# Windowed attention and a softplus layer on one core: later blocks' scores in three matmuls per query tile, a corrected plan with a table of due times, and the last store in pieces

## The chip, the core and the metric

The kernel runs on one core of one Trainium2 chip. Five engines of that core work side by side and wait for each other through semaphores: TensorE (PE, matrix products; the loads of its stationary operand are shown apart as PEld), VectorE (DVE), ScalarE (ACT), GpSimd (POOL) and SyncE (SP, which here only issues DMAs). The metric is device time of one launch in microseconds (us); three runs of the kernel before have a median of 963.94 us.

## The reference

Attention in a sliding window of 64 keys for 8 batches x 8 heads x 576 positions x 64 dimensions, and behind it a layer with softplus between two weight matrices, on the 4608 rows of 512 that the attention gives:

```python
scores = (q @ k.T) / sqrt(64)                 # masked to 0 <= pos_q - pos_k < 64
attn = softmax(scores);  x = attn @ v         # x: 4608 x 512
h = x @ w_in                                  # 512 x 2048
g = maximum(h, 0) + log1p(exp(-abs(h)))
out = g @ w_out                               # 2048 x 512
```

The precision is that of fp32. Most products run in a faster form of fp32 (fp32r), and for that each operand is split in a high part (the value rounded to that form) and a low part (what is left of it); three products, high by high, high by low and low by high, stand for one.

## The kernel before, in words

**Tiling.** The 4608 rows are 12 blocks of 384 (`TB`), numbered `g` in the order in which they are worked. A block has four pairs of heads (`hp`) and three query tiles of 128 rows. The inner width of 2048 is 16 slices `f` of 128. There are 192 steps of the layer: block 0 with slices 0 to 7, block 1 with all 16, block 0 with the rest, and then each later block with all 16. A step is an up product U (12 matmuls of 384 columns, L622), ACT's three passes and DVE's one for softplus (L626 to L634), the split of the result in `g0` and `g1` (L636, L637), and a down product D (9 matmuls of 512 columns, L646), which adds into three PSUM banks `ps_o`. U has two PSUM banks (`ps_h`), so the U after the next can start only when DVE's L634 has read the bank of this one. "U4 of the second pass" below is U for block 1 and slice 4.

**Weights.** They arrive as 64-bit words, 1 MB for a slice. `convert` makes fp32 of them and splits it: ACT L297, DVE L298, L300, L302, ACT L304, DVE L305. All 16 slices are converted once, at the start.

**Attention.** Blocks 0, 1 and 2 take their scores in full fp32 straight from q and k as loaded (L367); for blocks 0 and 1, PE also turns the probabilities and multiplies them with v (L487, L498). Blocks 3 to 11 (36 pairs of heads, 108 query tiles) split q and k: `q_hl` holds q's high parts on partitions 0 to 63 and its low parts on 64 to 127; `k_s[0]` and `k_s[1]` hold k's high and its low parts, each twice, on both halves. A query tile then takes four matmuls of 192 columns (L411): for either head one with `k_s[0]` and one with `k_s[1]`. Behind the scores stand DVE's row minima (L338), ACT's exponentials with their sums (L436), DVE's division (L451), the split of the probabilities (L527 to L532), a DMA that turns them, and the product with v (L590).

**Order.** Nothing is left to a scheduler: `arrange` plays the whole program through with a cost for each operation, a due time for each, and rules for the buffers (each `Ring` has so many places; an operation that opens a buffer waits for the users of the one whose place it takes). Whatever comes out is the order in which every engine's instructions are written. `latest` then makes new due times from the end backwards, and the best of 8 rounds is kept. PE, DVE, ACT and POOL each take their instructions strictly in that order; SP's DMAs too.

**Start.** `setup` makes masks on POOL and DVE. For block 0, the first 64 columns of k are zeroed on POOL as part of the load (L354), behind POOL's own masks and its memset of `v13` (L274).

**End.** Each finished block is copied out of its three PSUM banks (L681) and stored in two pieces, 512 KB and 256 KB (L684).

Of the kernel before, what the change touches and what calls it, by code (L numbers as in the profile page):

```python
# [8 lines left out]
F32 = mybir.dt.float32  # L9
# [6 lines left out]
P = 128  # L16
# [10 lines left out]
ROUNDS = 8  # L27
DOWN = 6.3
AHEAD = (1, 1, 8, 8)
APART = (4, 6, 18, 19)  # L30
STRETCH = 1.4
EARLY = 30
# [4 lines left out]
RESULT = {"PE": 0.25, "DVE": 0.12, "ACT": 0.15, "POOL": 0.2, "SP": 2.0}  # L37
BYTES_PER_US = 390e3
LAUNCH = 1.3
# [30 lines left out]
def arrange(ops, rings):  # L70
# [3 lines left out]
    free = {"PE": 0.0, "DVE": 5.0, "ACT": 2.1, "POOL": 0.8, "SP": 0.8}  # L74
    pipe = 2.2
# [7 lines left out]
    while len(order) < len(ops):  # L83
        best = None
        for e, waiting in open_ops.items():
# [21 lines left out]
            o = min((o for at, o in could if at <= t + 1e-9), key=lambda o: o.due)  # L107
# [4 lines left out]
        t, o = best  # L112
        o.start = t
        free[o.eng] = t + o.cost
        o.end = t + o.cost + RESULT[o.eng]
        if o.nbytes:
            pipe = max(pipe, t + o.cost + LAUNCH) + o.nbytes / BYTES_PER_US
            o.end = pipe + RESULT["SP"]
# [7 lines left out]
        for n in o.later:  # L126
            left[id(n)] -= 1
            ready_at[id(n)] = max(ready_at[id(n)], t + o.cost if n.eng == o.eng and not o.nbytes else o.end)
            if not left[id(n)]:
                open_ops[n.eng].append(n)  # L130
# [44 lines left out]
def window_attention_softplus_ffn(  # L175
# [107 lines left out]
    converted = {}  # L283

    def convert(f):
# [9 lines left out]
        a = add("SP", 0.45, lambda: nc.sync.dma_start(raw(), w_words[f]), opens=[raw], nbytes=1024 * 1024, name=f"load{f}")  # L295
# [18 lines left out]
    def attention(g, hp):  # L314
# [27 lines left out]
        if quad:  # L342
# [9 lines left out]
            def load_k():  # L352
                if skip:
                    nc.gpsimd.memset(qk(1)[:, 0:CH], 0.0)  # L354
                by.dma_start(qk(1)[:, skip:], kT[c0 : c0 + P, t0 - CH + skip : t0 + TB])
            lq = add("SP", 0.65, lambda: nc.sync.dma_start(qk(0), qT[c0 : c0 + P, rows_t]), deps=waits, opens=[slot],
                     uses=[two["q_in"], two["k_in"], *far], nbytes=192 * 1024, name=f"q{tag}")
            lk = add("ACT" if by is nc.scalar else "SP", 0.65, load_k, deps=waits, opens=[],
# [22 lines left out]
        else:  # L381
# [7 lines left out]
            for i, half in enumerate(heads):  # L389
# [4 lines left out]
            k_s = [buf(att, [P, 2, CH + TB], F32R, f"k{i}") for i in range(2)]  # L394
# [4 lines left out]
            kh = add("ACT", 0.84, lambda: nc.scalar.copy(k_s[0](), k_in()), deps=loads[1], opens=[k_s[0]], uses=[k_in], name=f"kh{tag}")  # L399
            kl = add("DVE", 1.11, lambda: tt(k_s[1](), k_in(), k_s[0]().bitcast(F32), ALU.subtract), deps=[kh], opens=[k_s[1]],  # L400
                     uses=[k_in, k_s[0]], name=f"kl{tag}")
# [343 lines left out]
    with tc.manual_schedule():  # L745
        setup()
        for o, at in best[1]:
            o.fn()
# [44 lines left out]
```

## Time and profile before

| | |
|---|---|
| median of three runs (lowest, highest) | 963.94 us (963.61, 964.43) |
| the profiled execution: its own time | 965.21 us |
| the profiled execution: its span, first to last instruction | 963.4 us |
| mean granted TensorE clock | 0.993 |
| HBM over the span | 74.58 MB read, 10.22 MB written, 88 GB/s |

The span is shorter than the execution's own time by 1.8 us, which lie outside the recorded instructions. PE, DVE, ACT and POOL rows give busy time; "waits" give the time in which an engine sat idle and what ended it; the "chain that ended last" follows the program back from its last instruction, at each step to whatever released it. A busy PE is not PE at its peak, since matmuls are pipelined and their records overlap: the pace is read from the chain, whose pieces do not overlap. The rows themselves are shown in the prediction.

### The profile page before, as it was taken

The page shows a single profiled execution, that of the slowest core. Times are in us where ns is not written, and L with a number is a line of the kernel's source. Part 1 is how long each engine was busy: PE and PEld are TensorE (multiplying, and loading weights), DVE is VectorE, ACT ScalarE, POOL GpSimd, SP SyncE. Part 2 cuts the span into 40 slices and gives each one's busy share as a digit, 9 for nine tenths or more (in the row PEclk, how much of TensorE's full clock was granted, in tenths as well). Part 3 has the DMA queues.
Part 4 walks back from the last instruction along what each step waited for, and adds up shares of the span by engine and source line. Part 5 has one row for each costly group of instructions (what it writes and reads, how often), then busy time and mean ns, then how long its engine had stood idle before and what let it go on. Part 6 is the DMA issues. An engine that isn't in the chain of part 4 may idle for free.

```text
span 963.4 us, 16889 instructions
## 1 busy us (share of the span) xinstructions
PE 939.7 (98%) x6128; PEld 848.6 (88%) x6128; DVE 784.6 (81%) x1760; ACT 740.5 (77%) x1685; POOL 4.5 (0%) x18
## 2 busy tenths in 40 slices
PE   5899999999999999999999999999999999999997
PEld 4678888999999999998999999999999999998996
DVE  7999977898798888889879889879888887975333
ACT  6899877888788788778878778778878887875443
POOL 1000000000000000000000000000000000000000
PEclk7999999999999999999999999999999999999999
DMA  9961225575347345344445535535635464521000
GB/s 364 422 231 44 61 71 121 131 178 124 90 129 138 98 139 116 94 117 128 122 99 145 137 76 145 132 89 140 127 86 150 116 111 99 148 52 34 34 1 33
DMA packets 196516, 117.37 MB, mean 122 GB/s; under 512 B 130192, under 2 KB 187536, under 8 KB 194384
## 3 DMA queue, kind: packets, MB, share of 16 engines
q1 hardware_dynamic: 196144, 115.90, 46.0%
q8 instruction: 48, 0.79, 0.4%
q10 hardware_dynamic: 288, 0.39, 0.1%
q14 instruction: 36, 0.29, 0.1%
HBM read 74.58 MB, written 10.22 MB: 88 GB/s over the span
## 4 chain that ended last, share of the span: by engine, by line
PE 91%; DVE 6%; ACT 1%; issue 1%; POOL 0%; POOLq 0%; ACTq 0%
PE ps_o L646 40%; PE ps_h L622 40%; PE ps_a L590 6%; PE ps_a L411 5%; DVE work L300 1%; DVE work L302 1%; DVE w L305 1%; ACT st L436 1%; DVE st L338 1%; DVE work L298 1%; DVE u L634 0%; DVE g L637 0%; PE ps_a L367 0%; DVE st L451 0%; DVE x L505 0%
## 5 line engine op out<-in xcount | busy, mean ns | idle before, releaser
L622 PE MATMUL ps_h<-x,w 128*128 128x384 f32 x2304 | 435.2, 338 | 4.2 <-DVE u L634 3.2
L646 PE MATMUL ps_o<-w,g 128*128 128x512 f32 x1728 | 424.9, 394 | 0.0
L622 PEld LDWEIGHTS ps_h<-x,w 128*128 128x128 f32 x2304 | 401.9, 188 | 15.0 <-DVE u L634 3.9
L646 PEld LDWEIGHTS ps_o<-w,g 128*128 128x128 f32 x1728 | 320.3, 188 | 60.4 <-ACT u L626 0.2
L626 ACT ACTIVATE u<-ps_h 128x384 f32<-128x384 f32 x192 | 93.8, 488 | 138.2 <-PE ps_h L622 134.9
L634 DVE SCALAR_TENSOR_TENSOR u<-ps_h,u 128x384 f32<-128x384 f32 x192 | 106.3, 554 | 95.8 <-ACT u L628 93.5
L436 ACT ACTIVATE st<-st,mn 128x128 f32<-128x128 f32 x288 | 111.7, 389 | 24.2 <-DVE st L428 19.1
L637 DVE TENSOR_TENSOR g<-u,g 128x384 fp32r<-128x384 f32 x192 | 106.3, 554 | 10.1 <-ACT g L636 5.8
L628 ACT ACTIVATE u<-u 128x384 f32<-128x384 f32 x192 | 100.9, 525 | 6.1
L627 ACT ACTIVATE u<-u 128x384 f32<-128x384 f32 x192 | 100.8, 525 | 6.1
L338 DVE CUSTOM_DVE_ANT_0 st<-ps_a,wide 128x192 f32<-128x192 f32 x176 | 53.3, 351 | 13.8 <-PE ps_a L411 13.8
L636 ACT CAST g<-u 128x384 fp32r<-128x384 f32 x112 | 56.5, 505 | 9.8 <-DVE u L634 9.0
L590 PEld LDWEIGHTS <-v 128*128 128x128 bf16 x1136 | 54.5, 98 | 9.6 <-issue 7.2
L590 PE MATMUL ps_a<-tr,v 128*128 128x128 bf16 (+1 forms) x1136 | 60.3, 211 | 0.0
L411 PEld LDWEIGHTS ps_a<-k,q_hl 128*128 128x128 f32 x432 | 56.3, 191 | 2.4
L411 PE MATMUL ps_a<-k,q_hl 128*128 128x192 f32 x432 | 55.9, 271 | 0.0
L436 ACT ACTIVATION_READ_ACCUMULATOR st<-st,mn 128x1 f32 x288 | 53.9, 187 | 0.0
L451 DVE TENSOR_TENSOR st<-st,sm 128x768 f32<-128x768 f32 x48 | 45.9, 955 | 0.9
L549 DVE TENSOR_TENSOR v_in<-v_in,v 128x896 f32<-128x896 f32 x40 | 43.5, 1089 | 3.5 <-ACT v L548 3.1
L551 DVE TENSOR_TENSOR v<-v_in,v 64x896 bf16<-64x896 f32 x40 | 43.6, 1090 | 3.1 <-ACT v L550 1.6
L599 DVE TENSOR_TENSOR xf<-ps_a,xf 64x384 f32<-64x384 f32 x80 | 43.8, 548 | 1.5
L597 ACT COPY xf<-ps_a 64x384 f32<-64x384 f32 x80 | 38.1, 476 | 4.9 <-PE ps_a L590 3.1
(77 smaller groups left out, 754.2 us busy)
## 6 DMA issues: line engine op xcount, KB each, us to landing
v_in<-in_v_dram SPq DMA_DIRECT2D x80, 224.0 KB, 3.4
raw<-in_w_words_dram SPq DMA_DIRECT2D x16, 1024.0 KB, 13.9
k_in<-in_kT_dram SPq DMA_DIRECT2D x72, 224.0 KB, 3.6
q_in<-in_qT_dram SPq DMA_DIRECT2D x72, 192.0 KB, 3.4
out_dram<-raw SPq DMA_DIRECT2D x12, 512.0 KB, 4.0
out_dram<-raw SPq DMA_DIRECT2D x12, 256.0 KB, 4.0
v_two<-in_v_dram SPq DMA_DIRECT2D x3, 768.0 KB, 10.8
q_two<-in_qT_dram SPq DMA_DIRECT2D x8, 192.0 KB, 8.4
```

What stands on the lines that cost most here:

```text
L338: nc.vector.tensor_tensor_reduce(st()[:, hh, j, 0:width], scores, m, QSCALE, 3.0e38, ALU.add, ALU.min, mn()[:, hh, j : j + 1])
L411: mm(spv[:, hh, :], q_hl()[:, hh, j * P : (j + 1) * P], k_s[i]()[:, hh, j * P : j * P + W], start=(hh == 0 and i == 0), stop=(hh == 1 and ...
L436: nc.scalar.activation(sv()[:, i, 0:P], sv()[:, i, 0:P], AF.Exp, bias=mn()[:, hh, j : j + 1], scale=-1.0, accum_out=sm()[:, i : i + 1],)
L590: mm(av()[:, osl], (v3() if s else v12())[:, c, hh, :, :], src, start=(i == 0), stop=(i == len(passes) - 1), skip_group_check=True,)
L622: mm(hps()[:, :TB], weight(0, a, f)[:, c * P : (c + 1) * P], x[b][c](), start=(i_mm == 0), stop=(i_mm == 3 * NC - 1))
L626: nc.scalar.activation(u(), hps()[:, :TB], AF.Abs)
L627: nc.scalar.activation(u(), u(), AF.Exp, scale=-1.0)
L628: nc.scalar.activation(u(), u(), AF.Ln, bias=1.0)
L634: m = add("DVE", 0.47, lambda: stt(u(), hps()[:, :TB], 0.0, u(), ALU.max, ALU.add), deps=[s], uses=[hps, u], name=f"m{g}.{f}")
L636: lambda: (nc.scalar.copy if by_act else nc.vector.tensor_copy)(gt[0](), u()), deps=[m], opens=[gt[0]], uses=[u], name=f"g0.{g}.{f}")
L637: lo = add("DVE", 0.47, lambda: tt(gt[1](), u(), gt[0]().bitcast(F32), ALU.subtract), deps=[h], opens=[gt[1]], uses=[u, gt[0]], name=f"g1. ...
L646: mm(acc[j](), gt[a]()[:, j * P : (j + 1) * P], weight(1, b, f), start=(first and i == 0), stop=(last and i == 2),)
```

## The change

Six edits, made together:

1. **Scores of blocks 3 to 11.** A new tile `diag` takes the place of `k_s[1]`: it holds k's low parts for head 0 on partitions 0 to 63 and for head 1 on 64 to 127, and zeros in the two other quarters, written once by POOL. A new tile `q_n` holds q's high parts of the two heads on the two halves. One matmul of 384 columns, `q_n` by `diag`, gives high by low for both heads, and two of 192 give the rest: three matmuls for a query tile instead of four. (The product of the two low parts, which the second matmul with `q_hl` added before, is no longer there.) ACT makes `q_n` with two copies of 64x384 for each pair of heads; DVE's one subtraction for `k_s[1]` becomes two of 64x448.
2. **Buffers.** `g1` has two places instead of three.
3. **Plan.** Other costs and latencies in `arrange` (a slower PE in the first 24 us, DMAs, SP's cost of an issue), ties broken by the order of making; and one more round that starts from a table `FIRST` of due times for some 380 operations of the start.
4. **Start.** The four memsets of k's first 64 columns are moved from POOL, where they were part of the load, to the front of DVE's order.
5. **End.** The last block's three banks are copied and stored apart, the last bank in two halves, by DVE with SP and by ACT with its own DMA queue (`finish`).
6. **Load of v.** One DMA of the start counts as 896 KB in the plan instead of 128.

```diff
+FIRST = {
+    0: 32.76, 1: 36.21, 2: 41.24, 3: 46.78, 4: 37.57, 5: 48.62, 6: 59.62, 7: 35.6, 8: 45.27, 9: 52.47, 10: 57.67,
...
+COLD, SLOW = 24.0, 1.22
-RESULT = {"PE": 0.25, "DVE": 0.12, "ACT": 0.15, "POOL": 0.2, "SP": 2.0}
-BYTES_PER_US = 390e3
-LAUNCH = 1.3
+RESULT = {"PE": 0.25, "DVE": 0.12, "ACT": 0.15, "POOL": 0.2, "SP": 0.1}
+BYTES_PER_US = 425e3
+LAUNCH = 2.8
...
-    free = {"PE": 0.0, "DVE": 5.0, "ACT": 2.1, "POOL": 0.8, "SP": 0.8}
-    pipe = 2.2
+    free = {"PE": 0.0, "DVE": 5.3, "ACT": 0.75, "POOL": 0.8, "SP": 0.75}
+    pipe = 0.0
...
+        cost = o.cost * SLOW if o.eng == "PE" and t < COLD else o.cost
...
+        for _, k_slot in qk_slots:
+            nc.vector.memset(k_slot[:, 0:CH], 0.0)
...
-                if skip:
-                    nc.gpsimd.memset(qk(1)[:, 0:CH], 0.0)
                 by.dma_start(qk(1)[:, skip:], kT[c0 : c0 + P, t0 - CH + skip : t0 + TB])
...
-            k_s = [buf(att, [P, 2, CH + TB], F32R, f"k{i}") for i in range(2)]
+            q_n = buf(att, [P, TB], F32R, "q_n")
+            k_s = buf(att, [P, 2, CH + TB], F32R, "k0")
+            k_d = held("diag", [None])
...
+            qn = [add("ACT", 0.4, lambda hh=hh, half=half: nc.scalar.copy(q_n()[half, :], q_in()[half, hh, :]), ...
...
-            kl = add("DVE", 1.11, lambda: tt(k_s[1](), k_in(), k_s[0]().bitcast(F32), ALU.subtract), ...
+            for hh, half in enumerate(heads):
+                k = add("DVE", 0.54, lambda hh=hh, half=half: tt(diag[0]()[half, hh, :], k_in()[half, hh, :],
+                                                                 k_s()[half, hh, :].bitcast(F32), ALU.subtract),
...
+                    mm(spv, q_n()[:, j * P : (j + 1) * P], diag[0]()[:, :, j * P : j * P + W], start=True, stop=False, ...)
                     for hh in range(2):
-                        for i in range(2):
-                            mm(
-                                spv[:, hh, :], q_hl()[:, hh, j * P : (j + 1) * P], k_s[i]()[:, hh, j * P : j * P + W],
-                                start=(hh == 0 and i == 0), stop=(hh == 1 and i == 1), skip_group_check=True,
-                            )
+                        mm(
+                            spv[:, hh, :], q_hl()[:, hh, j * P : (j + 1) * P], k_s()[:, hh, j * P : j * P + W],
+                            start=False, stop=(hh == 1), skip_group_check=True,
+                        )
...
+                def zero():
+                    for hh, half in enumerate(heads):
+                        nc.gpsimd.memset(diag[0]()[half, 1 - hh, :].bitcast(F32), 0.0)
...
+    def finish(d, rows, acc):
+        o = [buf(ff, [P, 1, DM], w_words.dtype, "raw", n=2) for _ in range(2)]
+        half = DM // 2
+        for j in range(NJ):
+            for part_of, eng in (((0, DM), "ACT"),) if j == 0 else (((0, DM), "DVE"),) if j == 1 else (((0, half), "DVE"), ((half, DM), "ACT")):
+                to, queue = (nc.scalar, nc.scalar if j == 2 else nc.sync) if eng == "ACT" else (nc.vector, nc.sync)
...
-        gt = [buf(ff, [P, TB], F32R, f"g{i}", n=3) for i in range(2)]
+        gt = [buf(ff, [P, TB], F32R, f"g{i}", n=3 - i) for i in range(2)]
...
+    for r in range(ROUNDS + bool(FIRST)):
+        if r == ROUNDS:
+            for i, o in enumerate(ops):
+                o.due = FIRST.get(i, best[2][i])
```

What this does to the order shows at three places. The first is PE where the scores of the first pair of heads of block 3 begin (`k_2025` is `k_s[0]`, `k_2031` is `k_s[1]`). Before, a query tile is four rows of 192 columns, behind the last matmul of a D:

```order
L646 MATMUL ps_o_1861<-w,g_2029 128x512 x2
L646 MATMUL ps_o_1861<-w,g_2050 128x512
L411 MATMUL ps_a<-k_2025,q_hl 128x192
L411 MATMUL ps_a<-k_2031,q_hl 128x192
L622 MATMUL ps_h<-x_0_0_323,w 128x384
```

Now it is one of 384 and two of 192, and the three query tiles of the pair no longer stand in one run: a D stands between the second and the third.

```order
L709 MATMUL ps_h<-x_3_0_410,w 128x384
L466 MATMUL ps_a<-diag,q_n 128x384
L468 MATMUL ps_a<-k_2005,q_hl 128x192 x2
L733 MATMUL ps_o_1849<-w,g_2070 128x512 x2
L733 MATMUL ps_o_1849<-w,g_2089 128x512
L656 MATMUL ps_a<-tr,v_2028 128x64
```

The second place is DVE in the second pass, in front of its pass over the U of slice 2 (the last row), which frees the PSUM bank for U4. `raw` are copies of block 0's half-finished sums, `w` is the last step of a slice's conversion. Before:

```order
L634 SCALAR_TENSOR_TENSOR u_1053<-ps_h_1021,u_1053 128x384
L637 TENSOR_TENSOR g1_1076<-u_1035,g0_1071 128x384
L681 COPY raw_1078<-ps_o0_524 128x512
L305 TENSOR_TENSOR w_1074<-work_1017,w_1074 128x1024
L637 TENSOR_TENSOR g1_1102<-u_1053,g0_1080 128x384
L681 COPY raw_1104<-ps_o2_532 128x512
L444 TENSOR_SCALAR sm_916<-sm_916 128x6
L634 SCALAR_TENSOR_TENSOR u_1098<-ps_h_1058,u_1098 128x384
```

Now work for the attention of block 2 stands there, moved ahead (its division L509, two steps of the split of its probabilities, and three minima of the next pair of heads, of which one is shown), and one `g1` (L724 for slice 1) has moved behind:

```order
L509 TENSOR_TENSOR st_81<-st_81,sm_1018 128x768
L771 COPY raw_1059<-ps_o0_564 128x512
L354 TENSOR_TENSOR w_1056<-work_937,w_1056 128x1024
L724 TENSOR_TENSOR g1_1083<-u_1036,g0_1061 128x384
L771 COPY raw_1085<-ps_o2_572 128x512
L721 SCALAR_TENSOR_TENSOR u_1078<-ps_h_1042,u_1078 128x384
L594 TENSOR_TENSOR st_81<-st_81,nat_1101 128x768
L598 COPY nat_1101<-nat_1101 128x12x64
L387 ISA st_81,mn_1125<-ps_a_1089,mask_q_92 128x128
L721 SCALAR_TENSOR_TENSOR u_1105<-ps_h_1064,u_1105 128x384
```

The third place is SP at the end of the program. `raw_10943` is the third bank of the last block, `raw_10941` the first two. Before, the small store is issued ahead of the large one:

```order
L523 DMA_TRANSPOSE tr_10233<-nat_10194 128x12x128 x2
L684 DMA out_0_dram<-raw_10468 128x512
L684 DMA out_0_dram<-raw_10466 128x2x512
L684 DMA out_0_dram<-raw_10943 128x512
L684 DMA out_0_dram<-raw_10941 128x2x512
```

Now the first two banks go out one by one, and half of the third behind them; the other half is on ACT's queue:

```order
L589 DMA_TRANSPOSE tr_10286<-nat_10241 128x12x128 x2
L774 DMA out_0_dram<-raw_10471 128x512
L774 DMA out_0_dram<-raw_10469 128x2x512
L695 DMA out_0_dram<-raw_10944 128x512 x2
L695 DMA out_0_dram<-raw_10947 128x256
```

More of the change, by code (lines that the diff above doesn't have):

```diff
@@ L127, in arrange @@
             left[id(n)] -= 1
-            ready_at[id(n)] = max(ready_at[id(n)], t + o.cost if n.eng == o.eng and not o.nbytes else o.end)
+            ready_at[id(n)] = max(ready_at[id(n)], t + cost if n.eng == o.eng and not o.nbytes else o.end)
             if not left[id(n)]:
@@ L398, in attention @@
                      deps=[qh], uses=[q_in, q_hl], name=f"ql{tag}")
[L399 to L401 removed]
+            qn = [add("ACT", 0.4, lambda hh=hh, half=half: nc.scalar.copy(q_n()[half, :], q_in()[half, hh, :]), deps=loads[0] + before_split,
+                      opens=[] if hh else [q_n], uses=[q_in, q_n] if hh else [q_in], name=f"qn{tag}") for hh, half in enumerate(heads)]
+            qn[1].deps.append(qn[0])
+            qn[0].later.append(qn[1])
+            kh = add("ACT", 0.84, lambda: nc.scalar.copy(k_s(), k_in()), deps=loads[1], opens=[k_s], uses=[k_in], name=f"kh{tag}")
+            kl, k = [], kh
+            for hh, half in enumerate(heads):
+                k = add("DVE", 0.54, lambda hh=hh, half=half: tt(diag[0]()[half, hh, :], k_in()[half, hh, :],
+                                                                 k_s()[half, hh, :].bitcast(F32), ALU.subtract),
+                        deps=[k, zeroed[0]], opens=[] if hh else [k_d], uses=[k_in, k_s, diag[0]] + ([k_d] if hh else []), name=f"kl{tag}")
+                kl.append(k)
             rdeps = []
@@ L418, in minima @@
                         scaled_min(hh, j, sp()[:, hh * W : (hh + 1) * W])
-                before = add("PE", 0.45, scores, deps=[qh, ql, kh, kl, before], opens=[sp] if j else [sp, st, mn], uses=[q_hl, *k_s], name=f"S{tag}")
+                before = add("PE", 0.4, scores, deps=[qh, ql, *qn, kh, *kl, before], opens=[sp] if j else [sp, st, mn],
+                             uses=[q_hl, q_n, k_s, k_d, diag[0]], name=f"S{tag}")
                 rdeps.append(add("DVE", 0.56, minima, deps=[before],
@@ L610, in window_attention_softplus_ffn, with view, take @@
     ups, downs, stores = [], [], []
+    def finish(d, rows, acc):
[4 more added lines that the diff above has]
+                to, queue = (nc.scalar, nc.scalar if j == 2 else nc.sync) if eng == "ACT" else (nc.vector, nc.sync)
+                a, b = part_of
+                def view(j=j, a=a, b=b):
+                    return o[j // 2]().bitcast(F32).rearrange("p m (j n) -> p (m j) n", n=DM)[:, j % 2, a:b]
+                def take(to=to, view=view, j=j, a=a, b=b):
+                    (to.copy if to is nc.scalar else to.tensor_copy)(view(), acc[j]()[:, a:b])
+                c = add(eng, 0.6 if b - a == DM else 0.35, take, deps=[d], opens=[o[j // 2]] if j % 2 == 0 and a == 0 else [],
+                        uses=[acc[j]] + ([] if j % 2 == 0 and a == 0 else [o[j // 2]]), name=f"end{j}")
+                st = add("ACT" if queue is nc.scalar else "SP", 0.45,
+                         lambda queue=queue, view=view, j=j, a=a, b=b: queue.dma_start(rows[j * P : (j + 1) * P, a:b], view()),
+                         deps=[c], uses=[o[j // 2]], nbytes=(b - a) * P * 4, name=f"store{j}")
+                stores.append((len(steps) - 1, st))
     def ffn(n, g, f, first, last):
@@ L740, in window_attention_softplus_ffn @@
         if best is None or end < best[0]:
-            best = (end, [(o, o.start) for o in order])
+            best = (end, order, [o.due for o in ops])
         latest(order, end)
```

41 lines of the change are left out of this document (25 added, 16 removed), and 40 rows, old and new, of the table FIRST.

## The prediction

> **What bounds the kernel now.** I read the chain that ended last first, then busy time by stretches, then the waits. The page's chain and its pieces around 91 us:
>
> ```profile
> PE 91%; DVE 6%; ACT 1%; issue 1%; POOL 0%; POOLq 0%; ACTq 0%
> ...
> 70.47 0.20 DVE st L338
> ...
> 90.72 0.44 DVE u L634
> 91.21 2.35 PE ps_h L622 x12
> 93.56 2.06 PE ps_o L646 x9
> ```
>
> Up to 91.21 us the chain runs mostly over DVE; from there to the last matmul it is PE alone. The piece at 91.21 is U4 of the second pass, held until DVE's L634 has read the bank that it needs. The same by stretches (columns: stretch, length, busy time of PE, PEld, DVE, ACT and POOL with instruction counts, PE clock, DMA share, GB/s):
>
> ```profile
> 0.00:6.82 6.82, 1.61 (x32) 1.61 (x36) 3.60 (x9) 1.28 (x1) 4.50 (x18) 1.00 0.76 250
> 6.82:24.00 17.18, 11.47 (x160) 9.29 (x153) 14.81 (x66) 15.31 (x59) 0.00 (x0) 0.70 1.03 409
> 24.00:91.20 67.20, 59.53 (x520) 49.25 (x514) 66.54 (x145) 59.91 (x143) 0.00 (x0) 1.00 0.59 235
> 91.20:168.00 76.80, 76.79 (x519) 68.29 (x520) 65.33 (x128) 62.76 (x132) 0.00 (x0) 1.00 0.38 93
> 168.00:900.00 732.00, 732.00 (x4625) 667.95 (x4624) 614.82 (x1378) 577.06 (x1305) 0.00 (x0) 1.00 0.49 116
> 900.00:958.30 58.30, 58.30 (x292) 52.21 (x290) 18.84 (x37) 24.22 (x47) 0.00 (x0) 1.00 0.00 1
> 958.30:963.40 5.10, 0.00 (x0) 0.00 (x0) 0.69 (x1) 0.00 (x0) 0.00 (x0) 0.77 0.42 154
> ```
>
> Three stages. **Start**, to 91.2 us: from 6.82 us on DVE is idle for only 2.37 + 0.66 = 3.0 us, so DVE sets the pace and PE waits. **Middle**, to 958.3: PE is never idle, so only less PE work helps. **Tail**: 5.1 us behind the last matmul. A gain is real if it shortens DVE's way to U4, PE's work behind U4, or the tail.
>
> **Scores (edit 1).** Pieces of the chain in the middle, all of one stretch in which PE waits for nothing:
>
> ```profile
> 177.28 1.32 PE ps_a L411 x12
> ...
> 188.40 2.06 PE ps_o L646 x9
> 190.46 2.08 PE ps_h L622 x12
> ```
>
> A 512-column matmul takes 2.06 / 9 = 0.229 us, one of 384 takes 2.08 / 12 = 0.173, one of 192 takes 1.32 / 12 = 0.110. The first two differ by 0.056 per 128 columns; by that slope alone 192 columns would take 0.173 - 0.084 = 0.089. The row says 0.110, so something besides the columns holds narrow matmuls, and the wide ones not. A query tile is 4 x 0.110 = 0.440 now and 0.173 + 2 x 0.110 = 0.393 after: 0.047 less, over 9 blocks x 4 pairs x 3 tiles = 108 tiles **-5.1 us**, all of it behind U4. No row shows a moving operand in two pieces (two heads of 192 out of a 448-wide tile); the 384-wide row is nearest. Ends: if the wide one costs as much as two narrow ones, nothing; if the narrow ones behind it fall to 0.089, 0.440 - 0.351 over 108 tiles, -9.6 us.
>
> The Trainium skill, page "TensorE: Matmul & The Clock Gate", section "Back-to-back issue gap", gives N / 2.4 + 2.5 ns as the pace of a matmul of N columns by itself, under which 768 columns cost nearly the same in three matmuls as in four. The 0.110 speaks against it here; by it the edit would give 0.3 us (108 times 2.5 ns, an estimate from that page).
>
> The copies for `q_n` cost ACT 72 more instructions; the two subtractions of 448 columns stand for one of 896 on DVE, and no cost is added.
>
> ```profile
> L601 ACT CAST x<-xf 128x384 fp32r<-128x384 f32 x40 | 20.3, 507 | 1.6 <-DVE xf L599 1.6
> L400 DVE TENSOR_TENSOR k<-k_in,k 128x896 fp32r<-128x896 f32 x36 | 39.0, 1083 | 2.4 <-ACT k L399 2.4
> ACT u L626 <- PE ps_h L622: 120.9, 72, 5.5
> ```
>
> 72 x 0.507 = 36.5 us against 732.00 - 577.06 = 155 us in which ACT is idle between 168 and 900, and most of ACT's waits there are for PE (the last row: us, times, longest), so ACT waits for the engine that sets the end. Ends: 0, and +36.5 if every copy delayed PE. Since PE is busy for 732.00 of 732.00 us beside it, I take a value close to the lower end, **+0.4 us**, a hundredth. Edit 2 belongs to this: with two `g1`, DVE's L637 waits for the D two steps back, and the minima and L634 queued behind it wait too, and for L634 the next U. D and U alternate in the chain, so that D is mostly done; I price it inside the 0.4.
>
> **Start (edits 3, 4 and 6).** The table moves instructions among about 90 us of DVE work; I sum DVE's way to U4.
>
> ```profile
> 0.77 0.87 ACTq L355 DMA_DIRECT2D k_two<-in_kT_dram  x2
> ...
> 2.08 1.84 DVE L269 COPY mask_q<-wide 64x128 bf16<-64x128 bf16 x1
> ...
> 2.28 1.59 POOL L274 MEMSET v<- 128x1792 bf16 x1
> ...
> 4.29 0.19 DVE L269 COPY mask_q<-wide 64x128 bf16<-64x128 bf16 x1
> ...
> 5.21 1.56 PE L367 MATMUL ps_a<-k_two,q_two 64*64 64x128 f32 x24 [5.21 <-POOL k_two L354]
> ...
> 6.82 0.29 DVE L338 CUSTOM_DVE_ANT_0 st<-ps_a,mask_q 128x128 f32<-128x128 f32 x1 [1.64 <-PE ps_a L367]
> ```
>
> ```profile
> k_two<-in_kT_dram ACTq DMA_DIRECT2D x1, 192.0 KB, 3.5
> ```
>
> (a) PE's first matmul waits for POOL's memset of k, which stands behind L274. With those memsets on DVE, in its idle 0.9 us before the masks, the late one is the load of k: 0.77 + 3.5 = 4.3 us instead of 5.21. DVE's masks are done at 5.2 us, so its first minimum moves from 6.82 to about 5.9: **-0.9 us** (ends: 0, if the load lands later; -1.6, DVE's whole idle time there).
>
> (b) Of the 3.0 us of DVE's idle time behind, the new order fills some: the first conversion (L298 to L302) now stands on DVE ahead of the third division, and its weights ahead of v on SP's queue. I take **-1.8 us**; ends 0 and -3.0.
>
> (c) Ahead of the L634 that frees U4's bank stand now one division, two steps of the split and three minima more, and one `g1` less:
>
> ```profile
> L451 DVE TENSOR_TENSOR st<-st,sm 128x768 f32<-128x768 f32 x48 | 45.9, 955 | 0.9
> L528 DVE TENSOR_TENSOR st<-st,nat 128x768 f32<-128x768 f32 x40 | 38.0, 950 | 1.2 <-ACT nat L527 1.1
> L532 DVE COPY nat<-nat 128x768 bf16<-128x768 bf16 x40 | 14.2, 354 | 0.3
> L637 DVE TENSOR_TENSOR g<-u,g 128x384 fp32r<-128x384 f32 x192 | 106.3, 554 | 10.1 <-ACT g L636 5.8 <-DVE g L636 0.5
> ```
>
> 0.955 + 0.950 + 0.354 + 3 x 0.20 (the chain's piece of L338) - 0.554 = **+2.3 us**. The PE work behind U4 is otherwise the same steps, so this is paid in full, unless a wait of PE elsewhere in the start is shorter by it.
>
> (d) POOL zeroes two quarters of `diag`, 64x448, when block 1's attention is done, at about 74 us, where DVE sets the pace.
>
> ```profile
> L274 POOL MEMSET v<- 128x1792 bf16 x1 | 1.6, 1592 | 0.0
> L354 POOL MEMSET k_two<- 128x64 f32 x2 | 0.2, 150 | 0.1
> ```
>
> By columns, the first row gives 448 / 1792 x 1.592 = 0.40 us, the second 7 x 0.150 = 1.05, each too low or too high; I take 0.5 each, 1.0 for both. The mask copy beside L274 took 1.84 us and the same copy later 0.19, so a copy on DVE can lose the whole of a POOL memset. Ends 0 and +1.0; I take half, **+0.5 us**. The Trainium skill, page "SBUF — State Buffer", section "Who interferes with whom", says that a DVE copy, cast or tensor_scalar in a two-port mode and a GpSimd instruction block each other for a whole instruction; the 1.84 agrees. By that rule the cost is the full +1.0 if a copy or L298 meets the memsets, and 0 if only operations with two inputs do.
>
> Start: -0.9 - 1.8 + 2.3 + 0.5 = +0.1 us. It goes nowhere, because what is saved in the first 24 us is spent on block 2's attention.
>
> **Tail (edit 5).**
>
> ```profile
> 957.64 0.59 ACT L681 COPY raw<-ps_o 128x512 f32<-128x512 f32 x1 [2.76 <-PE ps_o L646]
> 958.34 0.69 DVE L681 COPY raw<-ps_o 128x512 f32<-128x512 f32 x1 [0.69 <-PE ps_o L646]
> 959.06 0.81 SPq L684 DMA_DIRECT2D out_dram<-raw  x2
> ```
>
> ```profile
> out_dram<-raw SPq DMA_DIRECT2D x1, 512.0 KB, 3.1
> out_dram<-raw SPq DMA_DIRECT2D x1, 256.0 KB, 2.0
> ```
>
> Both stores are issued at 959.06, since the large one queues behind the small one; the large one lands 3.1 us after its issue, at about 962.5. In the new order the first stores go out once DVE has copied the second bank, at about 958.4, and the halves of the third at about 958.34 + 0.35 (half of 0.69) + one issue of 0.4 = 959.1, landing 2.0 later at 961.1 if nothing is ahead, or 0.66 earlier than now if all 768 KB pass at today's rate. Ends -0.6 and -1.4; I take **-0.8 us**.
>
> **Sum.** -5.1 + 0.4 + 0.1 - 0.8 = -5.4 us. Against the profiled execution (965.21 us; span 963.4 and 1.8 outside it) that is 959.8; the median of three runs is 963.94, so I forecast **958.5 us**.
>
> **Rivals.** *Columns alone count*, or the wide matmul in two pieces takes 0.220: the scores give 0, and the rest is -0.3 us: 963.6. For it: the middle's wide matmuls do go by columns. Against: the 0.110. *Narrow matmuls also speed up* to 0.089: -9.6 in place of -5.1 gives 954.0. *The start is not as summed*: PE's waits come later, at steps where DVE is nearly as late as at U4 (in 91.2 to 168 DVE is busy for 65.33 of 76.80 us), because the new order holds two `g1` and more attention early; one U lost, 2.08, gives 960.6, one U and one D, 4.1, 962.6; if instead the whole 3.0 us of idle time is filled and POOL costs nothing, 956.8. *Slower*: ACT takes the place of PE's freedom. The two `q_n` copies stand ahead of a softplus pass of ACT, L626, in the strict order; the L634 behind it then frees a bank late, and U waits. Price 2 x 0.507 = 1.0 us for each of 36 pairs. It decides from the point where the gain of 5.8 is eaten, at 6 pairs of 36, and gives over 0.2% more than before from 8; at 10 it gives 963.9 - 5.8 + 10.1 = 968.2. Against it stand ACT's 155 idle us. *The matmuls change and nothing else does what it says* is inside the first case's range.
>
> **How the numbers follow.** A measurement of this kernel can tell about 0.2%, 1.9 us, from no change. The forecast with the terms' smaller ends: 0.62 (955.5 to 961.5). Columns alone: 0.10. Narrow ones faster too: 0.08. Waits in the start: 0.12, half of it under 962.0. Slower: 0.08. Faster: 0.62 + 0.08 + 0.06 = 0.76; same 0.10 + 0.06 = 0.16; slower 0.08. The range from 955.0 to 963.0 leaves out the case of 954.0, the slower one and part of the columns case, about 2 in 10.
>
> **What would show it.** In the changed profile: chain pieces of the three score matmuls at 0.39 us a tile (0.35 or 0.44 under the rivals); PE's first matmul at 4.3 us; the last wait of PE near 91 us at U4 of the second pass; no idle PE between there and the last matmul; that matmul's end to the span's end 4.3 us. I am wrong if PE is idle in the middle or if the score tile keeps its 0.44.

## The result and the profile after

The changed kernel takes **975.17 us** (median of 4 runs, 974.43 to 976.93) against 963.78 before: ratio 1.0117, 95% interval 1.0102 to 1.0132. It is slower by 11.4 us, where 958.5 was forecast. Its profiled execution took 976.93 us with a span of 974.8.

Busy time by stretches of the changed kernel (columns as in the prediction; the third stretch ends where PE's last wait of the start ends, here at U3 of the second pass, and the sixth with the last matmul), and the shares of its chain that ended last:

```profile
0.00:6.82 6.82, 2.54 (x48) 2.46 (x48) 4.61 (x22) 1.89 (x4) 4.10 (x14) 1.00 0.74 244
6.82:24.00 17.18, 9.12 (x118) 7.25 (x111) 13.80 (x55) 13.66 (x53) 0.00 (x0) 0.60 1.02 403
24.00:91.48 67.48, 59.68 (x528) 50.52 (x527) 66.90 (x147) 59.09 (x141) 0.93 (x2) 0.95 0.58 237
91.48:168.00 76.52, 76.52 (x488) 68.36 (x489) 62.23 (x123) 61.67 (x130) 0.00 (x0) 1.00 0.33 76
168.00:900.00 732.00, 721.46 (x4499) 653.33 (x4498) 624.92 (x1410) 610.04 (x1372) 0.00 (x0) 1.00 0.51 117
900.00:970.03 70.03, 70.03 (x353) 63.05 (x351) 23.43 (x45) 31.41 (x62) 0.00 (x0) 1.00 0.03 12
970.03:974.78 4.75, 0.00 (x1) 0.00 (x0) 0.46 (x2) 0.37 (x1) 0.00 (x0) 0.81 0.46 166
```

```profile
PE 61%; DVE 18%; ACT 12%; DMA 4%; issue 4%; SPq 1%; ACTq 0%; DVEq 0%
```

Most of the loss is in the middle: PE, never idle there before, is idle for 732.00 - 721.46 = 10.5 us. The chain now runs over DVE, ACT and DMAs for a third of the span; before, it ran over PE alone from 91.21 us to the last matmul. What PE and ACT waited for between 168 and 900 us (total us, times, longest):

```profile
PE ps_a L656 <- DVE mn L387: 5.5, 6, 1.2
PE ps_a L656 <- DMA tr<-nat: 3.1, 3, 1.4
PE ps_h L709 <- DVE u L721: 1.7, 3, 0.6
ACT v L614 <- DMA v_in<-in_v_dram: 5.5, 6, 1.7
ACT k L452 <- DMA k_in<-in_kT_dram: 3.7, 4, 1.7
```

PE waits at the V products (L656): for the probabilities' transposition, or for the minima (L387) that must have read a score bank. ACT waits for loads. Before, no engine waited for a DMA there. ACT's longest waits for PE, though, are not for U, as before, but for the V product whose result it copies (`xf`). Here is that row in the changed kernel and then in old_plan, a kernel explained below that has edits 1, 2, 4 and 5 and none of this loss:

```profile
ACT xf L663 <- PE ps_a L656: 25.3, 25, 3.2
ACT xf L622 <- PE ps_a L615: 1.4, 2, 1.2
```

For a finer account I counted each matmul of the trace at its undisturbed pace (0.174 us for 384 columns, 0.2305 for 512, 0.111 for 192, 0.056 and 0.0285 for the bf16 ones of 128 and 64, 0.060 for those of the start) and took the sum from the time on the clock. What is left is time that PE has lost. Up to 168 us it is 20.3 us before and 22.5 after; from 168 to 900 us 5.3 and 20.2. So the 11.4 us between the two spans are +2.2 in the start, +14.9 in the middle, -5.2 of work (the sums are 932.6 and 927.4 us) and -0.4 in the tail. (With the paces rounded as printed here, the figures from 168 to 900 us come out 0.5 to 0.6 us higher in every kernel and both sums 0.7 lower; the differences stay.) A row of idle time leaves out about 0.16 us of what each wait costs, because a matmul's record runs on for that long past its pace (a 384-column one lasts 0.34 us in the record, at a pace of 0.174).

One execution each of tr_reserve, late_lead and the kernel before was disturbed (1150, 1149 and 1547 us) and is left out of the ratios; in late_lead it was the profiled one, so that kernel has no profile to read.

### The profile page after: what moved, and what is told of

It reads as the page before. It is cut to its first block, busy times and chain, and to the rows that moved or that the text cites. A ratio compares the mean times of both kernels' runs of the same rounds, so it can differ in the third digit from the quotient of the medians.

```text
span 974.8 us, 16868 instructions
## 1 busy us (share of the span) xinstructions
PE 939.3 (96%) x6020; PEld 845.0 (87%) x6020; DVE 796.4 (82%) x1800; ACT 778.1 (80%) x1758; POOL 5.0 (1%) x16
## 4 chain that ended last, share of the span: by engine, by line
PE 61%; DVE 18%; ACT 12%; DMA 4%; issue 4%; SPq 1%; ACTq 0%; DVEq 0%
PE ps_o L733 27%; PE ps_h L709 27%; PE ps_a L656 4%; DVE st L387 2%; DMA k_in<-in_kT_dram 2%; DVE g L724 2%; DVE u L721 2%; ACT u L714 2%; ACT st L494 2%; ACT u L713 2%; PE ps_a L466 1%; PE ps_a L468 1%; DVE work L349 1%; DVE w L354 1%; DVE work L351 1%
## 5 line engine op out<-in xcount | busy, mean ns | idle before, releaser
L709 PE MATMUL ps_h<-x,w 128*128 128x384 f32 x2304 | 430.4, 338 | 3.6 <-DVE u L721 2.8
L733 PE MATMUL ps_o<-w,g 128*128 128x512 f32 x1728 | 430.2, 395 | 0.0
L721 DVE SCALAR_TENSOR_TENSOR u<-ps_h,u 128x384 f32<-128x384 f32 x192 | 106.5, 555 | 72.9 <-ACT u L715 71.7
L724 DVE TENSOR_TENSOR g<-u,g 128x384 fp32r<-128x384 f32 x192 | 106.5, 555 | 16.6 <-ACT g L723 10.4
L656 PE MATMUL ps_a<-tr,v 128*128 128x128 bf16 (+1 forms) x1136 | 65.2, 211 | 8.5 <-DVE mn L387 5.5
L656 PEld LDWEIGHTS <-v 128*128 128x128 bf16 x1136 | 55.5, 98 | 20.0 <-issue 11.6
L387 DVE CUSTOM_DVE_ANT_0 st<-ps_a,wide 128x192 f32<-128x192 f32 x176 | 54.0, 350 | 1.8 <-PE ps_a L468 1.5
L455 DVE TENSOR_TENSOR diag<-k_in,k 64x448 fp32r<-64x448 f32 x72 | 44.5, 618 | 8.6 <-ACT k L452 7.5
L509 DVE TENSOR_TENSOR st<-st,sm 128x768 f32<-128x768 f32 x48 | 46.0, 958 | 1.5
L616 ACT CAST v<-v_in 128x896 bf16<-128x896 f32 x40 | 37.4, 934 | 6.7 <-DVE v_in L615 6.5
```

The costliest lines, as they stand in the source:

```text
L387: nc.vector.tensor_tensor_reduce(st()[:, hh, j, 0:width], scores, m, QSCALE, 3.0e38, ALU.add, ALU.min, mn()[:, hh, j : j + 1])
L509: nrm = add("DVE", 0.88, lambda: tt(pn(), pn(), sm().unsqueeze(2).to_broadcast([P, 2 * NJ, P]), ALU.mult), deps=[s], uses=[st, sm], name=f ...
L656: mm(av()[:, osl], (v3() if s else v12())[:, c, hh, :, :], src, start=(i == 0), stop=(i == len(passes) - 1), skip_group_check=True,)
L709: mm(hps()[:, :TB], weight(0, a, f)[:, c * P : (c + 1) * P], x[b][c](), start=(i_mm == 0), stop=(i_mm == 3 * NC - 1))
L721: m = add("DVE", 0.47, lambda: stt(u(), hps()[:, :TB], 0.0, u(), ALU.max, ALU.add), deps=[s], uses=[hps, u], name=f"m{g}.{f}")
L724: lo = add("DVE", 0.47, lambda: tt(gt[1](), u(), gt[0]().bitcast(F32), ALU.subtract), deps=[h], opens=[gt[1]], uses=[u, gt[0]], name=f"g1. ...
```

## The experiments

"Plan's end" is the end that the planner's own sum gives for the order it keeps: a number of the program, not of the chip. "Idle" is 732.00 us less PE's busy time from 168 to 900 us; "lost" is counted as above. Ratios are to the kernel before, run beside each.

| kernel | time, us | ratio, 95% | plan's end | idle | lost to 168 | lost 168 to 900 |
|---|---|---|---|---|---|---|
| before | 963.78 | 1 | 961.5 | 0 | 20.3 | 5.3 |
| after | 975.17 | 1.0117 (1.0102 to 1.0132) | 956.2 | 10.5 | 22.5 | 20.2 |
| plan_alone | 968.71 | 1.0050 (1.0035 to 1.0065) | 962.4 | 1.6 | 20.4 | 9.0 |
| g1_two | 967.35 | 1.0035 (1.0022 to 1.0048) | 964.7 | 0 | 22.4 | 4.7 |
| no_table | 964.24 | 1.0006 (0.9997 to 1.0015) | 958.0 | 2.0 | 23.7 | 8.6 |
| old_plan | **958.86** | 0.9949 (0.9933 to 0.9966) | 957.6 | 0 | 20.1 | 4.8 |
| dma_old | 962.97 | 0.9989 (0.9979 to 0.9998) | 958.7 | 1.9 | 20.6 | 8.5 |
| old_dma_new | 970.91 | 1.0072 (1.0057 to 1.0087) | 955.0 | 7.1 | 22.5 | 14.3 |
| tr_reserve | 964.42 | 1.0003 (0.9994 to 1.0013) | 956.3 | 3.6 | 20.2 | 10.2 |
| old_costs | 961.20 | 0.9970 (0.9958 to 0.9981) | 955.6 | 0 | 22.5 | 5.6 |
| loads_early | 969.73 | 1.0063 (1.0047 to 1.0078) | as after | 6.9 | 20.9 | 15.6 |
| qn_one | 967.40 | 1.0034 (1.0021 to 1.0047) | as after | 5.0 | 20.6 | 12.1 |
| early_one | 963.99 | 0.9998 (0.9989 to 1.0007) | as after | 1.9 | 20.4 | 8.7 |
| late_lead | 963.75 | 0.9998 (0.9988 to 1.0007) | as old_plan | | | |
| old_one | 958.47 | 0.9942 (0.9926 to 0.9959) | as old_plan | 0 | 20.4 | 4.2 |
| qn_more | 966.66 | 1.0025 (1.0016 to 1.0035) | as old_plan | 3.8 | 20.1 | 12.4 |
| qn_twice | 983.78 | 1.0203 (1.0187 to 1.0219) | as old_plan | 17.4 | 20.1 | 29.5 |

### Which part of the change

**plan_alone**: the kernel before with only the new costs of edit 3 and 6 (no table).

```diff
-RESULT = {"PE": 0.25, "DVE": 0.12, "ACT": 0.15, "POOL": 0.2, "SP": 2.0}
-BYTES_PER_US = 390e3
-LAUNCH = 1.3
+RESULT = {"PE": 0.25, "DVE": 0.12, "ACT": 0.15, "POOL": 0.2, "SP": 0.1}
+BYTES_PER_US = 425e3
+LAUNCH = 2.8
...
```

> The kernel before with the change's plan costs only (DMA latency and rate, SP's costs, slower cold PE, PE's and ACT's first free times, tie break left out, no table): scores in four matmuls, three places for g1, old store. Theory A (the plan's costs put loads and the work behind them too late): PE is idle in 168 to 900 us by 5 us or more and the time is 968 to 973 us. Theory B (the edit to the scores itself, with two copies more on ACT, two subtractions of 0.62 us on DVE and two places for g1, leaves too little slack in the middle): PE idle under 1 us there, the time within 2 us of 963.8.

**old_plan**: the changed kernel with those costs as before and an empty table; edits 1, 2, 4 and 5 stay. **no_table**: the changed kernel with `FIRST = {}`. **g1_two**: the kernel before with two places for `g1`.

> The change with the costs of the plan before and without the table: three score matmuls, two places for g1, memsets of k on DVE, last store in pieces. Theory A: the middle is without idle PE again, the time is 957 to 960 us (5.1 us for the scores and 0.8 for the store under 963.8). Theory B: PE idle in the middle by 8 us or more, the time at 968 us or above.

> The change with its own costs, without the table of due times. Theories A and B: the middle stays as in the change, about 10 us of idle PE between 168 and 900 us, the time 972 to 978 us. A third theory, C (the extra round from the table, whose due times fit another plan, is what loosens the middle): idle PE there under 3 us, the time 957 to 962 us.

> The kernel before with two places for g1 instead of three, planned anew with its own costs. Theory A: within 2 us of 963.8. Theory B, if the ring of g1 is what takes the slack: 968 us or more and DVE's L637 waiting for PE's L646 by several us; if the ring is not it, within 2 us of 963.8.

The costs alone make the old kernel slower by 4.75 us. That is the time of theory A, with less idle PE than it asked for (1.6 us, not 5). Without these costs and without the table the other edits give 958.86, close to the 958.5 that was forecast for all six. The row of old_plan from 168 to 900 us:

```profile
168.00:900.00 732.00, 732.00 (x4544) 667.19 (x4543) 626.78 (x1419) 615.47 (x1381) 0.00 (x0) 1.00 0.49 116
```

ACT has more to do here than in the changed kernel's row, and PE is never idle: the edits do not need the loss. no_table came between the expectations. With the table it is 11 us more, though the planner's sum is 1.8 us less. g1_two missed too: its middle is as before, and 2.1 of its 3.4 us are lost ahead of 168 us by another order of the start, so a new plan by itself moves this kernel by a few us.

### Which cost of the plan

By the figures before, a transposition of 384 KB (in the plan) counts 1.45 + 1.3 + 1.0 + 2.0 = 5.8 us from the start of its issue to its landing and a load of 224 KB 4.5. By the new ones it is 2.8 + 0.93 = 3.7 and 2.8 + 0.54 = 3.3. The DMA rows of the changed kernel, medians in us from issue to landing:

```profile
v_in<-in_v_dram SPq DMA_DIRECT2D x80, 224.0 KB, 4.3
k_in<-in_kT_dram SPq DMA_DIRECT2D x72, 224.0 KB, 3.7
q_in<-in_qT_dram SPq DMA_DIRECT2D x72, 192.0 KB, 4.6
tr<-nat SPq DMA_TRANSPOSE x80, 3.4
```

The old figures left a reserve of 2.4 us on a transposition and one of up to 0.8 us on a load of k or v; the new ones leave 0.3 on a transposition and lie below all three loads. The Trainium skill, page "DMA: Bandwidth & Descriptors", section "Anatomy of one DMA — SWDGE (gpsimd) path", gives 2.0 us + bytes / 436e3 for another path, by which an estimate for 224 KB is 2.5 us; the two rows of that size are 1.2 and 1.8 us above it.

**dma_old**: the changed kernel with only these three figures as before. Its planner tries the table's round, but keeps one of its own, so the table is not in use. **old_dma_new**: old_plan with only these three as in the change.

> The changed kernel with its table and its other new costs, and only the three figures of a landing as before (launch 1.3 counted behind the issue, 390e3 bytes per us, 2.0 us behind the last byte). The planner then keeps a round of its own, and not the table's. Theory A: no engine waits for a load in the middle, PE idle under 1 us between 168 and 900 us, time 957 to 961. Rival (the other new costs, such as the cold clock, the engines' free times and the shorter issues, are what loosened the middle): 962 to 968.

> The kernel old_plan with only the three figures of a landing as in the change. Theory A: loads land within 0.5 us of their use in several places, PE idle 1 to 8 us between 168 and 900 us, time 961 to 968. Rival (the other new costs): no PE idle in the middle, time 957 to 961.

The three figures alone make old_plan 12 us slower, more than the 961 to 968 expected. Few loads are late in old_dma_new: 3 of 215 land under 0.5 us ahead of their reader, but 7 of 74 transpositions do. With the figures put back, dma_old is 12 us faster than the changed kernel, in the range of the rival. This does not show that the figures are worth 12 us there, because the table's round is gone too: against no_table, which has the new figures and no table either, it is 1.3 us, and both lose the same in the middle (8.5 and 8.6 us).

**tr_reserve**: the changed kernel with its costs and table, and a reserve for transpositions alone. In the plan:

```diff
             o.end = pipe = max(pipe, t + LAUNCH) + o.nbytes / BYTES_PER_US
+            if o.name[:2] == "tr":
+                o.end += 2.0
```

> The changed kernel, with its table and its costs, and 2.0 us added in the plan behind the landing of a transposition only (3.7 us from issue to landing becomes 5.7, as in the plan of before); the planner keeps the table's round. Theory A in its second form (the reserve that matters is the one behind the transpositions, which stand at the end of each pair's softmax): transpositions land 3 us or more ahead of their use in the median, 5 at least; PE's idle time between 168 and 900 us falls from 10.5 us to 3 or less, 960 to 966. Rival (the table itself makes the middle tight): 970 or more.

10.8 us come back with the table in use. From landing to first reader, a transposition now has 7.6 us in the median of 74 (3.7 in the changed kernel, where 8 of 74 landed under 0.5 us ahead; none does here). So neither the table nor the missing reserve costs 11 us by itself beside the other new costs: with the table and the reserve it is 964.42, without either 964.24, and only the table without the reserve takes 975.17. Beside the old costs, the missing figures cost 12 us without any table (old_dma_new). What a lost reserve costs hangs on the order that the planner falls on. The row of tr_reserve from 168 to 900 us:

```profile
168.00:900.00 732.00, 728.42 (x4552) 661.81 (x4551) 630.64 (x1416) 615.47 (x1378) 0.00 (x0) 1.00 0.48 117
```

**old_costs**: old_plan with 0.51 and 0.62 us as costs of a `q_n` copy and a subtraction, and 1.8 us in place of 2.0 behind a landing.

> The kernel old_plan with the plan's costs of the score edit as the trace has them (a copy of q_n 0.51 us in place of 0.4, a subtraction onto the diagonal 0.62 in place of 0.54) and 1.8 us in place of 2.0 behind a landing. By its own sum the plan ends at 955.6 us, where old_plan's ends at 957.6. If a reserve of that size is kept, the time follows the plan's sum as it did there: 955 to 959. If plans with a lower sum are ones with less slack and lose it on the chip: 960 or more.

PE is not idle in the middle, but 2.4 us more are lost in the start: another order, no gain.

### One thing at a time, in a fixed order

A new plan moves everything, so the next kernels keep the order that was planned and change one thing in it. In the changed kernel, the place where PE waits looks so (ACT, DVE and PE between 378 and 385 us; start, length, engine, line, what, idle time ahead of it):

```profile
378.31 1.03 ACT L448 CAST q_n<-q_in 64x384 fp32r<-64x384 f32 x2
379.37 0.49 ACT L713 ACTIVATE u<-ps_h 128x384 f32<-128x384 f32 x1
...
381.94 0.52 ACT L715 ACTIVATE u<-u 128x384 f32<-128x384 f32 x1
...
382.50 0.56 DVE L721 SCALAR_TENSOR_TENSOR u<-ps_h,u 128x384 f32<-128x384 f32 x1 [0.94 <-ACT u L715]
382.98 0.55 DVE L724 TENSOR_TENSOR g<-u,g 128x384 fp32r<-128x384 f32 x1
383.44 0.35 DVE L387 CUSTOM_DVE_ANT_0 st<-ps_a,wide 128x192 f32<-128x192 f32 x1
...
384.13 0.85 PE L656 MATMUL ps_a<-tr,v 128*128 128x64 bf16 x14 [1.18 <-DVE mn L387]
```

The two copies stand on ACT ahead of the softplus of two U; DVE's L721 waits 0.94 us for it, L724 and the minima queue behind L721, and PE's V product waits 1.18 us for the minima. ACT was late already: 10 us earlier it had waited for a load of k:

```profile
368.39 0.94 ACT L452 CAST k<-k_in 128x896 fp32r<-128x896 f32 x1 [0.80 <-DMA k_in<-in_kT_dram]
```

Two causes, then, that can be taken away one by one.

**loads_early**: each load of q, k and v that the plan issues after 150 us up to 4 us earlier in SP's queue, as far as its buffer is free.

```diff
+        if o.eng == "SP" and o.name[0] in "qkv" and 100 * 1024 < o.nbytes < 300 * 1024 and o.start > 150.0:
+            free = max([u.end for u in o.freed] + [d.end for d in o.deps if d.eng != "SP"] + [0.0])
...
+            key = max(free + 0.2, o.start - 4.0)
```

**qn_one**: one copy of `q_n` in place of two. The second head's high parts are left out; its rows take the first head's.

```diff
+            qn[0].fn, qn[1].fn = (lambda: nc.scalar.copy(q_n(), q_in()[:, 0, :])), (lambda: None)
```

**early_one**: both.

> The changed kernel with the order it has, but each load of q, k and v of blocks 2 and later is written up to 4 us earlier in the queue of SP, as far as its buffer is free by the plan; what PE, ACT, DVE and POOL run, and in which order, is the same, and so are the transpositions. Theory A (loads are issued too late, because the new costs count 3.3 us from issue to landing and nothing behind it): the loads land 3 to 4 us sooner, the 16 of 71 k_in loads that land under 0.5 us ahead of their use fall to 5 or fewer, PE's 10.5 us idle between 168 and 900 us fall to 5 or less, time 966 to 971. Theory B (ACT and DVE carry the score edit's added work with too little slack): the loads land sooner and the time stays within 2 us of 975. Theory D (transpositions, whose place depends on ACT and DVE, are what is late): the k_in waits go, the waits on transpositions and their time stay, 972 to 975.

> The changed kernel with the order it has, on every engine and in every queue, and one thing taken out: of the two copies that fill q_n for a pair of heads (510 ns each on ACT) the first writes all 128 rows from the first head's q, and the second is left out, so the products with the lower parts take a wrong q for half of the rows. ACT has 18 us less to do. Theory A (only the lateness of DMAs costs): within 2 us of 975.2. Theory B (ACT and DVE are full, so that each 0.1 us over the plan's cost is handed on): PE's idle time between 168 and 900 us falls by 3 us or more, 966 to 972.

> loads_early and qn_one together: the loads of q, k and v up to 4 us earlier in SP's queue, and one copy of q_n in place of two (half of the rows of q_n take a wrong q). loads_early alone was 969.7. If the two causes add, 961 to 967. If the loads' lead was all that could be had, 968 to 970.

Their rows from 168 to 900 us, in this order:

```profile
168.00:900.00 732.00, 725.10 (x4523) 658.04 (x4522) 625.15 (x1412) 611.58 (x1373) 0.00 (x0) 1.00 0.50 116
```

```profile
168.00:900.00 732.00, 727.05 (x4542) 660.67 (x4542) 627.02 (x1416) 592.17 (x1340) 0.00 (x0) 1.00 0.50 117
```

```profile
168.00:900.00 732.00, 730.14 (x4560) 664.36 (x4559) 628.45 (x1420) 593.51 (x1343) 0.00 (x0) 1.00 0.50 117
```

Earlier loads are worth 5.4 us, half the copies 7.8, both 11.2: nearly the sum, 13.2. Both theories held in time (in loads_early idle PE fell to 6.9 us only, not to 5); neither alone explains the loss. The loads of k, which in the changed kernel had a median of 4.4 us from landing to first reader and 16 of 71 under 0.5, had 7.0 and none in loads_early. Its waits for `mn` stayed (4.7 us in 6), as a cause on ACT would have it.

The same two things were then done to the plan that has a reserve. **late_lead**: old_plan with its loads written up to 6 us later. **qn_more**, **qn_twice**: one or both copies of `q_n` done twice. **old_one**: one copy in place of two, as in qn_one.

> What loads_late and late_mid were meant to be: old_plan in the very order of the plan that it keeps (those two wrote out the planner's last round, which the planner had thrown away, so they say nothing of a lead), with each load of q, k and v of blocks 2 and later written up to 6 us later in SP's queue, no later than 3.4 us ahead of its reader by the plan. All engines but SP run what old_plan runs, in its order. If a short lead costs by itself what it cost in the changed kernel (5.4 us): PE idle 2 us or more between 168 and 900 us, 963 to 968. If the rest of the plan's slack takes it up: PE idle under 1 us, within 1.5 us of 958.9.

> The kernel old_plan in its own order, each copy of q_n done twice, so that ACT has 36.7 us more to do (the values don't change). Reserve theory: the middle takes it up, PE idle between 168 and 900 us under 2 us, time within 2 us of 958.9. If q_n's time on ACT is a cost whatever the order (in the changed kernel 18 us of it were worth 7.8 us): 964 or more.

> old_plan in its own order with one of the two copies of q_n done twice: ACT has 18.4 us more to do (qn_twice, with 36.7 us more, took 983.8, 24.9 us above old_plan). If ACT's slack in old_plan is a fixed amount that qn_twice used up and went over: less than half of 24.9, 960 to 968. If each us on ACT costs 0.7 us from the first: 971 or more.

> old_plan in its own order with one copy of q_n for a pair instead of two, as in qn_one (half of the rows of q_n take a wrong q): ACT has 18.4 us less to do. As PE is never idle between 168 and 900 us in old_plan, nothing is to be had there: within 1 us of 958.9, where the same cut was worth 7.8 us in the changed kernel. If ACT's time is a cost whatever the order: 952 or less.

Late loads alone cost old_plan 4.9 us: a short lead is a cost in this order too. Only loads planned after 150 us were moved; which engine then waits is not shown. qn_twice went against the theory that a reserve takes the copies up. ACT's time is a curve: 18 us less gives -0.4 us (the executions of the two overlap, so this is not told from nothing), 18 us more +7.8, 37 us more +24.9. So old_plan's slack on ACT ends close to where the change puts it. In the changed kernel's order, with DMAs late as well, the same 18 us are worth 7.8 us: there the slack is gone. The row of qn_twice:

```profile
168.00:900.00 732.00, 714.60 (x4399) 641.75 (x4398) 615.12 (x1399) 639.16 (x1428) 0.00 (x0) 1.00 0.48 115
```

ACT is busy for 87% of the stretch and idle for 93 us, and still PE is idle for 17.4 us.

**loads_late** was meant as late_lead, **late_mid** as the same with the start untouched (959.5 to 963.5 us expected, or 964 and more), and **late_twice** as late_mid and qn_twice together (the sum of their costs expected, or 2 us and more above it). All three have their instructions in the order of the planner's last round, not of the one that old_plan keeps (plan's end 977.9 in place of 957.6). They took 983.69, 982.46 and 1012.41 us, some 43 us of them lost ahead of 168 us, and say nothing of a lead.

> The kernel old_plan with the order it has, but each load of q, k and v of blocks 2 and later is written up to 6 us later in the queue of SP, no later than 3.4 us ahead of the operation that reads it by the plan. Theory A: a lead like that of the changed kernel is enough by itself to make PE idle in the middle, 3 us or more between 168 and 900 us where old_plan has none, and the time is 962 to 970. Theory B: the engines' slack decides, the loads still land ahead of their use, time within 1.5 us of 958.9.

## Why the prediction was wrong, step by step

The step that failed is the middle: "PE is never idle, so only less PE work helps" was read from the old order and kept for the new one. By it the plan's new costs were priced at nothing from 168 to 900 us and the copies of `q_n` at 0.4 us. PE lost 14.9 us more there than before.

- **Scores, -5.1: right.** The chain's pieces of two query tiles in the changed kernel:

```profile
381.49 0.17 PE ps_a L466
381.66 0.20 PE ps_a L468 x2
381.87 0.20 PE ps_a L466
382.06 0.20 PE ps_a L468 x2
```

  From 381.49 to 382.26 that is 0.385 us a tile, where 0.393 was expected. By the starts of its matmuls, a tile behind a wide matmul takes 0.377 us and one behind another tile 0.400 (medians; before, 0.424 and 0.446): 0.046 to 0.047 less, as forecast. The two prices in the sum were both a little off and make up for each other: the pair of narrow ones takes 0.201, not 0.220, and the wide one behind a narrow one 0.198, not 0.173. Behind a wide one it takes 0.175, so the moving operand in two pieces costs no more than one piece. PE's work is 5.2 us less, and old_plan, 5.1 us below before, shows that it is got.
- **`q_n` on ACT, +0.4: this term failed in the changed order.** It read "PE is busy for 732.00 of 732.00 us beside it" as cover and took a hundredth of 36.5 us. Full PE in the old profile shows only that its waits were hidden with the old plan's reserve; it does not say how much more would be. Half the copies are worth 7.8 us in the changed order; in old_plan's they are worth 0.4, so there the term held. (The row of 120.9 us that it read for the middle is of the whole run; from 168 to 900 us that wait is 103.3 us in 64.) The prediction's own end of +36.5 was never reached, but its slower rival (the copies ahead of a softplus pass, L634 late, then PE) is what the trace at 378 us shows, with the minima's bank in place of U's. It was given 0.08 and a price of 4.3 us net. The prediction also added no cost for two subtractions in place of one; they took 1.24 us a pair of heads against 1.083, 5.5 us more on DVE over 36 pairs, and what that costs was not tried.
- **The plan's new costs in the middle: left out, and the loss comes with them.** They were priced only through the order of the start. All of the loss against old_plan, 16.3 us, comes with them and the table. It has no row on how far ahead of their use loads and transpositions landed (before 10.4 us in the median for k and 7.8 for a transposition, from landing to first reader), though the diff takes 2 us off a planned landing. In the changed order, loads written earlier give 5.4 us. In new orders, the reserve for transpositions alone gives 10.8, and the three figures alone cost old_plan 12.
- **Two `g1`: right in the middle** (g1_two's is as before), though the new plan that they bring lost 2.1 us in the start.
- **Start, +0.1: right in two of four terms.** Rows of PE and DVE, and the chain's piece of U4:

```profile
4.28 1.56 PE L414 MATMUL ps_a<-k_two,q_two 64*64 64x128 f32 x24 [4.28 <-DMA k_two<-in_kT_dram]
...
90.88 0.55 DVE L721 SCALAR_TENSOR_TENSOR u<-ps_h,u 128x384 f32<-128x384 f32 x1
91.46 0.96 DVE L594 TENSOR_TENSOR st<-st,nat 128x768 f32<-128x768 f32 x1
...
93.23 0.55 DVE L721 SCALAR_TENSOR_TENSOR u<-ps_h,u 128x384 f32<-128x384 f32 x1
...
93.84 2.35 PE ps_h L709 x12
```

  PE's first matmul stands at 4.28 us (4.3 forecast). The U that PE waits for last, at 91.48 us, is U3, not U4: the L721 of slice 2 stands behind the steps of the split and the minima, ends at 93.8 us, and U4 starts at 93.84, where it started at 91.21 before. In the three kernels that keep this start's order it starts at 91.4 to 92.1. DVE's first minimum came 0.9 us sooner, as forecast, and its added work, 2.2 to 2.6 us up to U4, is near the 2.8 of (c) and (d). Its idle time behind the first minimum was to fall by 1.8 us; it fell by 0.25 to 1.1 in those three and rose by 0.9 here. The profiled execution lost 2.2 us more than before by 168 us, but the three kernels that keep its start's order lost only 0.1 to 0.6 more, so most of the 2.2 is that execution's own. Its clock from 6.82 to 24 us was 0.60, and 0.70 before; whether that is why is not shown, since of the three the one with a clock of 0.70 there lost only 0.3 to 0.5 us more than the two with 1.00. POOL's two memsets took 0.93 us (1.0 forecast). Beside them DVE's L347 took 1.06 us here in place of 0.69; in the three others they ran beside L349 and L351, which took no longer than usual.
- **Tail, -0.8: half.** From the last matmul to the end it is 4.75 us, not 4.3. The end's timeline, and the DMA rows of its last two stores (KB each, median us from issue to landing):

```profile
970.10 1.30 SPq L695 DMA_DIRECT2D out_dram<-raw  x3
970.53 0.37 ACT L690 COPY raw<-ps_o 128x256 f32<-128x256 f32 x1 [1.25 <-DVE raw L690]
970.93 0.38 ACTq L695 DMA_DIRECT2D out_dram<-raw  x1
```

```profile
out_dram<-raw ACTq DMA_DIRECT2D x1, 128.0 KB, 2.4
out_dram<-raw SPq DMA_DIRECT2D x1, 128.0 KB, 2.5
```

  A store of 128 KB lands 2.4 to 2.5 us after its issue, where the sum took the 2.0 of one of 256 KB. In most of the later kernels with these stores the tail is 4.5 us.

What stays open: early_one is still 5.1 us above old_plan. Its transpositions were not moved, since their place hangs on ACT and DVE, and 3 of 74 still land under 0.5 us ahead of their use (argued, not tried). ACT's waits for the V product point the same way: between 168 and 900 us they are 35.0 us in early_one, and 25 to 32 us in every other kernel with the score edit and without the reserve, but 0 to 3.4 us in those with it. They take ACT's idle time without making PE idle by themselves (no_table has 25.7 us of them and 2.0 us of idle PE); no run took them away alone. Why the table's round in particular fell on such an order was not settled either.

## What to carry to other kernels

A latency in a planner is also its safety margin. In the changed kernel 196 of 215 loads and 23 of 74 transpositions took longer from issue to landing than the planner's new figures, and where queues run in strict order such lateness can be handed on. When costs are corrected, put the reserve back as a number of its own, and do not trust a lower sum: here the orders with sums of 955.0 and 956.2 us took 970.9 and 975.2, and one with 957.6 took 958.9. And a profile in which the limiting engine is never idle bounds what cutting other engines' work can gain; what adding to them costs is found by adding it, in the same order.

## What the runs showed of the hardware

Splitting an operation over the two partition halves is paid per instruction. These groups of the changed kernel give busy us, mean ns of one:

```profile
L455 DVE TENSOR_TENSOR diag<-k_in,k 64x448 fp32r<-64x448 f32 x72 | 44.5, 618 | 8.6 <-ACT k L452 7.5
L448 ACT CAST q_n<-q_in 64x384 fp32r<-64x384 f32 x72 | 36.7, 510 | 0.5
```

Two subtractions of 448 columns take 1.24 us where one of 896 took 1.083, and a copy on 64 partitions takes 510 ns, as long as one on 128 (507). The Trainium skill, page "VectorE: DVE Perf Modes", section "The TRN2 errata — SBUF-src ops pay a fixed extra latency per instruction", has formulas by which an estimate is (448 + 151) / 0.96 = 624 ns for the first and (224 + 384) / 1.2 = 507 ns for the second; the rows agree. So the second copy of `q_n` costs as much as the first, though each fills half a tile.

What a narrow matmul costs depends on the one ahead of it. From its start to the next one's start, a 192-column matmul took 0.089 us behind a wide one, and behind another narrow one 0.111 before the change and 0.1125 after it; the 384-column one of the scores took 0.175 behind a wide one and 0.198 behind a narrow one (medians of the changed kernel).
